# Scale block first, the first chunk's key product in token halves, PSUM as one tile of eight banks, and a new order of work, in a fused attention and token-mixer kernel

## The chip, the core and the metric

The kernel runs on one core of one Trainium2 chip. It is one launch that reads all its inputs from HBM and writes the whole output back. The metric is device microseconds of that launch, the median of several runs; lower is better. The engines named below are PE (matrix products; its weight loads have a row of their own, PEld), DVE (vector work), ACT (activations and copies), POOL (GpSimd) and SP (it issues most DMAs). Each engine works through its own queue strictly in the order in which the program was written; an instruction that waits holds up everything behind it on its engine.

## What is computed

A block of 2048 tokens of width 512 (`x`, bf16) passes two branches. Six modulation rows of 512 come from a conditioning vector: shift `sa`, scale `ca` and gate `ga` for the first branch, `sb`, `cb` and `gb` for the second.

```python
mod = (_silu(c) @ w_mod).reshape(1, 6, 1, -1)      # sa, ca, ga, sb, cb, gb
h = _layernorm(x) * (1 + ca) + sa
# 32 heads of 16; each token sees itself and 7 earlier ones, 2 apart
q, k, v = heads(h @ wqkv)
logits = einsum('bhsd,bhswd->bhsw', q, gathered(k)) * 16 ** -0.5
o = einsum('bhsw,bhswd->bhsd', softmax(masked(logits)), gathered(v))
x = x + ga * (o @ wo)
h = _layernorm(_layernorm(x) * (1 + cb) + sb)
u = gelu(einsum('bsd,sf->bdf', h, w1) + b1)        # mixes tokens, 2048 -> 1792
x = x + gb * transpose(einsum('bdf,fs->bds', u, w2) + b2)
```

## The kernel before

The 2048 tokens are worked in four chunks of 512 (`build_chunk`, chunk number first in the names below), each of four tiles of 128 tokens. For a chunk the steps are:

- `ln1s` and `ln1n`: statistics and normalization of a token tile. `rstd` (ACT) and `nb` (DVE or POOL) lie between them.
- `tr`: PE transposes the normalized tiles into PSUM. `hT` copies them out with the scale `1 + ca` (`a1col`) and the shift `sa` (`sacol`) applied, one per 128 features (kt 0 to 3).
- `qkvq`, `qkvk`, `qkvv`: the three products, each of 16 matmuls of 512 columns; `evq`, `evk`, `evv` copy them to SBUF.
- `qk` (DVE, four big products of 4096 elements per partition), `red` (PE sums them), `max`, `sub`, `exp`, `sum`, `rb`, `smul`: the softmax. `a2` and `a2ev` spread the weights.
- `vd`: 16 SBUF-to-SBUF DMAs make shifted copies of v. `pv` (DVE, four more big products), `pvacc` (PE) and `oev` give the attention output.
- `wo` (PE), `x1ev` (ACT or DVE) and `x1sq` (ACT): output product, residual and its statistics. When `x1ev` runs on ACT, PE adds the residual with a fifth matmul against the identity; on DVE the residual is an operand and four matmuls are enough. The gate `ga` is multiplied into `wo` beforehand by four `gmul`.
- `t`, `aff`, `ln3s`, `h3`: the second pair of normalizations.

The token mixer follows. `mlp1_0` multiplies `w1` with the first two chunks (8 token tiles), `park0` stores the half sums, `mlp1_1` does the last two chunks: its parts ending in `_0` need chunk 2's `h3`, those ending in `_4` chunk 3's. Then come `gadd`, `gelu`, `gbm`, the product `mlp2` with `w2`, `xb` (residual and bias, one per token tile), `fin` and the stores. `modcols` is the product that gives `sa` and `ca` as columns, `modrows` gives the other four rows, `bc` spreads each over the partitions by a DMA, and `biascols` transposes the biases. `warm` are matmuls whose result nobody reads.

The order of all this is written out: `ORDER` (line 27) is one list of names, and the program records each step in that order, so it sets the order in every engine's queue and in SP's. A letter behind a name picks the engine (v is DVE, a is ACT, g is POOL), a digit the PSUM buffer. PSUM is four tiles of two banks (lines 272 to 277). All instructions are recorded through one helper, so the profile's line is L184 for all of them; the tile names tell them apart. `_Graph` (line 98) checks that the order respects the data.

Of the kernel before, what the change touches and what calls it, by code (L numbers as in the profile page):

```python
# [980 lines left out]
```

## Time and profile before

| quantity | value |
|---|---|
| runs | 198.53, 198.63, 199.68 us; median 198.63 |
| span of the profiled execution, first to last instruction | 197.0 us |
| median run less that span | 1.6 us |
| PE busy | 190.1 us (97%), 1289 matmuls |
| DVE busy | 153.5 us (78%), 198 instructions |
| ACT busy | 123.4 us (63%) |
| POOL busy | 18.0 us (9%) |
| granted TensorE clock | 0.998 of full speed over the span |

The profile was taken of one execution, and its only own time is the span; no time with the launch around it is given for that execution apart. Times in the trace count from the span's start. A row of the timeline gives start, length, engine, operation, written tile, read tiles, shapes and how many instructions were merged; in brackets stands the idle time before it and what ended it. Successive instructions overlap by some hundredths of a microsecond, so work in a full queue is counted from start to start. PE's rows overlap more: a matmul of 512 columns lasts 379 ns, but the next starts after 0.215 us.

### The profile page before, as it was taken

How to read it: one execution, taken by the hardware profiler on the slowest of the kernel's cores; microseconds unless marked ns; L12 is line 12 of the kernel's file. 1: busy time of each engine (PE TensorE's matmuls, PEld its weight loads, DVE VectorE, ACT ScalarE, POOL GpSimd, SP SyncE). 2: the span in 40 equal slices, each digit the busy share in tenths (PEclk: the TensorE clock that was granted, in tenths of full speed). 3: DMA queues.
4: the chain of work that ended last, by engine and by line, in shares of the span. 5: the costliest groups of instructions: out<-in, count | busy, mean ns of one | idle time of the engine just before them, and what ended most of it. 6: DMA issues, size and time to landing. Idle time of an engine off the chain costs nothing.

```text
span 197.0 us, 3408 instructions
## 1 busy us (share of the span) xinstructions
PE 190.1 (97%) x1289; PEld 88.2 (45%) x1289; DVE 153.5 (78%) x198; ACT 123.4 (63%) x242; POOL 18.0 (9%) x46
## 2 busy tenths in 40 slices
PE   7889999999999999999999999999999999999994
PEld 2546545445443435433434444444444444444452
DVE  1699989999999999999999999928776127261463
ACT  5498999999999999993769999917541000000000
POOL 7003040090000004300000011000000000000000
PEclk9999999999999999999999999999999999999999
DMA  6999978507994994693999999990000871720112
GB/s 182 369 312 318 302 195 177 120 14 180 171 196 99 270 201 84 187 289 106 174 206 290 234 295 292 292 273 4 0 0 0 229 200 68 199 81 26 57 53 80
DMA packets 45348, 33.59 MB, mean 171 GB/s; under 512 B 5396, under 2 KB 42772, under 8 KB 45332
## 3 DMA queue, kind: packets, MB, share of 16 engines
q1 hardware_dynamic: 44908, 32.82, 67.2%
q10 hardware_dynamic: 424, 0.56, 1.0%
q8 instruction: 10, 0.16, 0.4%
q14 instruction: 6, 0.05, 0.1%
HBM read 22.03 MB, written 2.10 MB: 122 GB/s over the span
## 4 chain that ended last, share of the span: by engine, by line
PE 64%; DVE 12%; DMA 11%; ACT 5%; SPq 3%; issue 2%; ACTq 0%; DVEq 0%
PE ps L184 64%; DMA vD<-v_c 5%; DMA w_q<-in_A_wqkv_dram 4%; SPq L184 3%; DVE pvb L184 3%; DVE prod L184 3%; DMA vD<-in_w_mod_dram 3%; DVE st L184 2%; ACT n_sb L184 1%; DVE h L184 1%; ACT hTb L184 1%; DVE gT L184 1%; ACT v_c L184 1%; DVE ee L184 1%; DVE nm L184 1%
## 5 line engine op out<-in xcount | busy, mean ns | idle before, releaser
L184 DVE TENSOR_TENSOR pvb<-a2sb,vD 128x4096 bf16<-128x4096 bf16 x16 | 36.0, 2284 | 0.2 <-issue 0.2
L184 PE MATMUL ps<-h,wst 128*128 128x512 bf16 x128 | 29.5, 379 | 0.0
L184 DVE TENSOR_TENSOR prod<-q_sb,k_c 128x4096 bf16<-128x4096 bf16 x9 | 20.4, 2285 | 0.1
L184 PEld LDWEIGHTS <-wst 128*128 128x128 bf16 x128 | 12.1, 98 | 16.0 <-issue 1.7
L184 PE MATMUL ps<-gT,vD 128*128 128x512 bf16 x84 | 19.1, 379 | 0.0
L184 PE MATMUL ps<-hTb,w_q 128*128 128x512 bf16 x64 | 15.1, 381 | 1.0 <-DMA w_q<-in_A_wqkv_dram 0.7
L184 DVE TENSOR_TENSOR q_sb<-ps,q_sb 128x512 bf16<-128x512 f32 x8 | 5.4, 687 | 13.6 <-PE ps L184 13.6
L184 PE MATMUL ps<-woq,o_sb 128*128 128x512 bf16 x64 | 15.8, 379 | 0.0
L184 PEld LDWEIGHTS <-w_q 128*128 128x128 bf16 x96 | 9.9, 109 | 12.6 <-issue 2.5
L184 PE MATMUL ps<-hTb,w_v 128*128 128x512 bf16 x64 | 15.0, 380 | 0.0
L184 PE MATMUL ps<-hTb,w_k 128*128 128x512 bf16 x64 | 15.0, 380 | 0.0
L184 DVE TENSOR_TENSOR k_c<-ps,k_c 128x512 bf16<-128x512 f32 (+2 forms) x9 | 5.6, 629 | 11.7 <-PE ps L184 11.7
L184 PEld LDWEIGHTS <-o_sb 128*128 128x128 bf16 x106 | 9.7, 98 | 10.5 <-issue 0.4
L184 PEld LDWEIGHTS <-vD 128*128 128x128 bf16 x116 | 9.2, 97 | 11.4 <-DMA vD<-in_w_mod_dram 1.5
L184 PE MATMUL ps<-gT,pvb 128*128 128x512 bf16 x56 | 12.9, 379 | 0.0
L184 PEld LDWEIGHTS <-w_k 128*128 128x128 bf16 x80 | 8.7, 111 | 8.9 <-issue 0.8
L184 PE MATMUL ps<-gT,prod 128*128 128x512 bf16 x56 | 12.2, 379 | 0.0
L184 PEld LDWEIGHTS <-w_v 128*128 128x128 bf16 x80 | 8.3, 111 | 8.2 <-issue 1.3
L184 ACT ACTIVATE junk<-xx,su 128x512 bf16<-128x512 bf16 x16 | 11.5, 720 | 0.5 <-DVE xx L184 0.2
L184 DVE BATCH_NORM_STATS2 st<-xx 128x6 f32<-128x512 bf16 x11 | 7.4, 671 | 4.7 <-DMA xx<-in_A_x_dram 4.7
L184 ACT ACTIVATE hTb<-ps,sacol,a1col 128x512 bf16<-128x512 bf16 x13 | 9.6, 782 | 0.5 <-PE ps L184 0.5
L184 DVE TENSOR_TENSOR gT<-q_sb,k_c 128x4096 bf16<-128x4096 bf16 x4 | 9.1, 2284 | 0.0
(113 smaller groups left out, 315.1 us busy)
## 6 DMA issues: line engine op xcount, KB each, us to landing
vD<-v_c SPq DMA_DIRECT2D x64, 131.5 KB, 4.6
wst<-in_B_w_dram SPq DMA_DIRECT2D x8, 512.0 KB, 6.1
vD<-in_B_w_dram SPq DMA_DIRECT2D x3, 896.0 KB, 7.3
wst<-in_w_mod_dram SPq DMA_DIRECT2D x4, 512.0 KB, 9.3
prod<-in_B_w_dram SPq DMA_DIRECT2D x2, 896.0 KB, 11.0
pvb<-in_B_w_dram SPq DMA_DIRECT2D x2, 896.0 KB, 8.1
xx<-in_A_x_dram SPq DMA_DIRECT2D x4, 256.0 KB, 4.7
xx<-in_A_x_dram SPq DMA_DIRECT2D x2, 512.0 KB, 7.7
```

Source lines behind the costliest of these rows:

```text
L184: r = fn(*a, **k)
```

## The change

The new kernel computes the same. Its parts:

1. **Scale block first.** The loads of the scale `ca` come right behind the first x tiles (`ld_ca0`, `ld_ca1`, 256 KB each), then the key weights, and the shift `sa` only then (`ld_sa`, 512 KB). Before, shift and scale came together (`ld_wmodA`, `ld_wmodB`, 512 KB each). `modcols` becomes `colsa` and, later, `colss`.
2. **The first chunk's keys.** `hk` copies the transposed tiles out of PSUM with the scale alone, for 256 tokens at a time. The key product of chunk 0 loops over kt outermost and over the two token halves: 8 groups of 4 matmuls of 256 columns, instead of 16 matmuls of 512.
3. **Shift as bias.** `kbias` multiplies the shift with the key weights (16 one-column matmuls); `evk0` adds it while it copies. For queries and values of chunk 0, `hadd` adds the shift to the scaled tiles.
4. **PSUM** is one tile of eight banks. A step takes one bank or two neighbours; before, each took a pair.
5. **New order** of everything, with other engines for some steps. In the table the steps on POOL go from 17 to 25: 7 `ln1n` instead of 5, all 4 `gmul` instead of 1, 4 `t` instead of 3, 5 `h3` instead of 3. `x1ev` goes to ACT 13 times instead of 9. `xb1`, `xb0` and `xb3` move from the end of the program to between the last chunks' steps on DVE. `warm2`, `warm3` and `warm4` (2, 3 and 3 matmuls) now stand among the chunks' products.

On ACT the start reads as follows before: sums of the scale and shift columns out of PSUM, one `hT`, then the statistics of chunk 1.

```order
L184 ACTIVATE lv_0_130<-mv_0_126,epscol 128x2
L184 ACTIVATE rs_0_136<-lv_0_130 128x2
L184 ACTIVATE sacol<-ps_61 128x4
L184 ACTIVATE a1col<-ps_61 128x4
L184 ACTIVATE hTb<-ps_63,sacol,a1col 128x512
L184 ACTIVATE junk,mv_1_127<-xx 128x512
L184 ACTIVATE junk,mv_1_127<-xx,mv_1_127 128x512
```

The same place on ACT in the new kernel (`gT` holds the scaled tiles, `sabf` and `sacol` the shift, `kbcol` the keys' bias):

```order
L187 ACTIVATE n_sb<-xx,nb_0_141,rs_0_135 128x512
L187 ACTIVATE gT<-ps,a1col 128x256 x2
L187 ACTIVATE sabf<-ps 128x4
L187 ACTIVATE sacol<-ps 128x4
L187 ACTIVATE junk,mv_1_126<-xx 128x512
L187 ACTIVATE junk,mv_1_126<-xx,mv_1_126 128x512
L187 ACTIVATE kbcol<-ps 128x4
L187 ACTIVATE hTb<-gT,sacol 128x512
```

The shift's columns come later than before, and between them and the first finished `hTb` tile stand a statistics step of chunk 1 and the copy of the bias.

POOL's queue behind its constants, before (`h_96` and `h_95` are the two chunks' buffers of the second normalization, `h_66` is `h3`):

```order
L184 TENSOR_SCALAR n_sb<-xx,rs_1_137,nb_1_143 128x512 x2
L184 TENSOR_SCALAR n_sb<-xx,rs_0_136,nb_0_142 128x512 x3
L184 TENSOR_TENSOR woq<-woq,ga_bc 128x512
L184 TENSOR_SCALAR h_96<-xx,rs_1_139,nb_1_145 128x512 x3
L184 TENSOR_SCALAR h_66<-h_95,rs_0_140,nb_0_146 128x512 x2
```

And in the new kernel (`h_93`, `h_92` and `h_63` are those three):

```order
L187 TENSOR_SCALAR n_sb<-xx,rs_1_136,nb_1_142 128x512 x3
L187 TENSOR_SCALAR n_sb<-xx,rs_0_135,nb_0_141 128x512 x2
L187 TENSOR_TENSOR woq<-woq,ga_bc 128x512 x4
L187 TENSOR_SCALAR h_93<-xx,rs_1_138,nb_1_144 128x512 x3
L187 TENSOR_SCALAR h_63<-h_92,rs_0_139,nb_0_145 128x512 x2
L187 TENSOR_SCALAR h_92<-xx,rs_0_137,nb_0_143 128x512
```

All four multiplications of `wo` by the gate now stand in POOL's queue, where there was one; three of them left DVE.

On DVE, the stretch around the last `pv` products reads like this before (the products `pvb<-`, three residual sums `xx,su<-`, then the second normalization):

```order
L184 TENSOR_TENSOR ee_83<-ee_83,rb 128x1024
L184 TENSOR_TENSOR pvb<-a2sb_84,vD_92 128x4096
L184 TENSOR_TENSOR pvb<-a2sb_85,vD_90 128x4096 x2
L184 SCALAR_TENSOR_TENSOR xx,su_0_148<-ps_61,xx 128x512
L184 SCALAR_TENSOR_TENSOR xx,su_0_148<-ps_62,xx 128x512
L184 SCALAR_TENSOR_TENSOR xx,su_0_148<-ps_64,xx 128x512
L184 TENSOR_TENSOR pvb<-a2sb_85,vD_91 128x4096
L184 SCALAR_TENSOR_TENSOR nb_0_144<-su_0_148,rs_0_138 128x4
L184 TENSOR_SCALAR h_95<-xx,rs_0_138,nb_0_144 128x512
```

And in the new kernel (`q_sb<-gb_bc` rows are `xb1` and `xb0`, the CAST is `oev2_3`):

```order
L187 TENSOR_TENSOR ee_80<-ee_80,rb 128x1024
L187 SCALAR_TENSOR_TENSOR q_sb_72<-gb_bc,b2col,xx 128x512
L187 CAST o_sb<-ps 128x1024
L187 TENSOR_TENSOR pvb<-a2sb_82,vD_87 128x4096 x2
L187 TENSOR_TENSOR pvb<-a2sb_82,vD_88 128x4096 x2
L187 SCALAR_TENSOR_TENSOR nb_0_143<-su_0_147,rs_0_137 128x4
L187 TENSOR_SCALAR h_92<-xx,rs_0_137,nb_0_143 128x512
L187 SCALAR_TENSOR_TENSOR q_sb_71<-gb_bc,b2col,xx 128x512
```

The three residual sums left DVE there, and two `xb` and one copy out of PSUM joined it.

The diff, cut to its core (of `ORDER` one line on each side):

```diff
-consts ld_x00 consts2 ld_c warm0:0 ld_x02 ld_wmodA act_table ld_wmodB ld_w1a ld_x1a cps:1 warm1:2 ld_w1b silu_exp
+consts ld_c ld_x00 ld_x02 ld_ca0 ld_ca1 act_table ld_wk0 ln1s1:v ld_wk2 consts2 warm0:0 ln1s0:v cps:0 silu_exp warm1:1
...
-    WARM=(4, 4, 4, 5, 4),
+    WARM=(4, 4, 2, 3, 3),
...
-    NPS = 4
-    ps = [psp.tile([P, 2, 512], F32, name=f"ps{i}") for i in range(NPS)]
+    NPS = 8
+    ps = psp.tile([P, NPS, 512], F32, name="ps")
...
+    for kh in range(2):
+        dma(wmodc[1][:, 2 * kh:2 * kh + 2, :], wmod_view[:, 2 * kh:2 * kh + 2, D:2 * D], D * P * 2 * 2, [],
+            vdk[0][2 * kh:2 * kh + 2], f"ld_ca{kh}", "act" if kh == 0 else "sp")
...
+    dma(wmodc[0], wmod_view[:, :, 0:D], KT * D * P * 2, [], vdk[0][4:], "ld_sa")
...
+    mod_cols(1, range(KT), "colsa")
...
+    mod_cols(0, range(KT), "colss")
...
+    def f_kb():
+        for j in range(4):
+            for kt in range(KT):
+                nc.tensor.matmul(bank(sl_kb, 0)[:, j:j + 1], lhsT=_ap(w_p[1][:, kt, j:j + 1], [[4, P]]),
+                                 rhs=sabf[:, kt:kt + 1], start=(kt == 0), stop=(kt == KT - 1), skip_group_check=True)
...
+                if ch == 0:
+                    dst = hraw[:, kt, t0:t1]
+                    alts = [("act", _act(n_, 1), lambda dst=dst, src=src, sc_=sc_: nc.scalar.activation(
+                                dst, src(), ACT.Identity, scale=sc_)),
...
+        if ch == 0:
+            for kt in range(KT):
+                rk_ = [("gT", 2 + kt, g0) for (g0, g1) in parts]
+                G.add_any([("dve", 0.25, lambda kt=kt: nc.vector.tensor_scalar(
+                                hT[:, kt, :], hraw[:, kt, :], sacol[:, kt:kt + 1], None, op0=ALU.add)),
...
+            for (g0, g1) in parts:
+                for kt in range(KT):
+                    def f(kt=kt, g0=g0, g1=g1):
+                        for j in range(4):
+                            nc.tensor.matmul(bank(sk[j], 0)[:, g0 * P:g1 * P], lhsT=_ap(w_p[1][:, kt, j:j + 1], [[4, P]]),
+                                             rhs=hraw[:, kt, g0 * P:g1 * P], start=(kt == 0), stop=(kt == KT - 1))
...
+            for j in range(4):
+                dst = k_c[b][:, j, PAD:PAD + C]
+                G.add_any([("act", _act(C), lambda j=j, dst=dst: nc.scalar.activation(
+                                dst, bank(sk[j], 0), ACT.Identity, bias=kbcol[:, j:j + 1])),
```

299 lines of the change are left out of this document (168 added, 131 removed).

## The prediction, on record before the changed kernel was run

> **What bounds the kernel now.** I read the page first, then the chain of waits, then stretches of time, then the engines' timelines. The page's busy row puts PE at 97%, and DVE's slices are full until the 28th of 40.
>
> ```profile
> PE 190.1 (97%) x1289; PEld 88.2 (45%) x1289; DVE 153.5 (78%) x198; ACT 123.4 (63%) x242; POOL 18.0 (9%) x46
> DVE  1699989999999999999999999928776127261463
> ```
>
> The chain (start, length, what) tells which of the two sets the end: a load until 14.7 us, PE, a mixed middle, and PE again to the end.
>
> ```profile
> 6.71 7.94 DMA w_q<-in_A_wqkv_dram
> ...
> 14.70 19.33 PE ps L184 x145
> ...
> 86.30 106.59 PE ps L184 x585
> ```
>
> The stretches show how full the queues are (length, then PE, PEld, DVE, ACT, POOL busy).
>
> ```profile
> 86.30:128.28 41.98, 41.98 (x284) 17.66 (x284) 40.48 (x58) 34.31 (x68) 1.19 (x3) 1.00 1.02 238
> 128.28:194.09 65.81, 65.81 (x319) 30.51 (x317) 33.79 (x53) 9.91 (x15) 0.00 (x0) 1.00 0.32 89
> 14.70:128.28 113.58, 112.42 (x886) 52.04 (x887) 110.75 (x122) 103.88 (x199) 14.12 (x15) 1.00 0.87 204
> ```
>
> From 14.70 on PE idles only 113.58 - 112.42 = 1.16 us, and after 128.28 not at all. DVE is as full: 110.75 of 113.58. At 128.28 PE starts `mlp1_1`'s parts that need chunk 3's `h3`; DVE has written the last of these 0.56 us earlier:
>
> ```profile
> 126.64 1.08 DVE L184 TENSOR_SCALAR h<-h,mv,rs 128x512 bf16<-128x512 bf16 x3
> 128.28 5.99 PE L184 MATMUL ps<-h,wst 128*128 128x512 bf16 x27
> ```
>
> So 128.28 is a gate with two queues before it, both nearly full. Behind it stand the same 20 groups of `mlp1_1` and the same 16 `mlp2` in both programs, 65.81 us without a gap. The forecast is how far the gate moves: the later of PE's and DVE's arrivals.
>
> **The change, part by part.** The start first.
>
> ```profile
> 5.66 0.69 DVE L184 BATCH_NORM_STATS2 st<-xx 128x6 f32<-128x512 bf16 x1 [1.26 <-DMA xx<-in_A_x_dram]
> 9.81 1.45 DVE L184 TENSOR_SCALAR hTb<-ps,a1col,sacol 128x512 bf16<-128x512 bf16 x3 [1.10 <-PE ps L184]
> 16.67 4.49 DVE L184 TENSOR_TENSOR prod<-q_sb,k_c 128x4096 bf16<-128x4096 bf16 x2
> 6.75 0.55 PE L184 MATMUL ps<-sc,vD 128*128 128x1 bf16 x16 [0.69 <-DMA vD<-in_w_mod_dram]
> 10.40 3.61 PE L184 MATMUL ps<-hTb,w_k 128*128 128x512 bf16 x16
> 14.70 3.65 PE L184 MATMUL ps<-hTb,w_q 128*128 128x512 bf16 x16 [0.69 <-DMA w_q<-in_A_wqkv_dram]
> 10.24 0.62 ACT L184 ACTIVATE junk<-xx 128x512 bf16<-128x512 bf16 x1
> 10.99 0.72 ACT L184 ACTIVATE junk<-xx,mv 128x512 bf16<-128x512 bf16 x1
> 16.44 0.83 ACT L184 ACTIVATE n_sb<-xx,nb,rs 128x512 bf16<-128x512 bf16 x1
> ```
>
> One 512-column matmul costs (3.61 - 0.38) / 15 = 0.215 us, a one-column one 0.025. DVE's new queue has `ln1s3`, whose x landed at 5.66, ahead of the silu product: 5.66 + 0.85 + 0.13 = 6.6. `colsa` (16 x 0.025) and the copy of the scale bring it to 7.3. A 256-column `hk` lies between half of 0.54 and 0.54; I take 0.3, since the width is what is halved. The key product so starts near 7.8, not 10.40. Its 32 half-width matmuls cost the same 3.45, but behind it now stand `colss` and `kbias` (0.4 each), the second half's transposes (0.45) and `biascols` (0.14): PE is free at 12.6. The queries must wait longer, for `hadd`. Tile 2's statistics on ACT take 1.5 from 5.66, then come rstd 0.5 and the norm 0.8: near 8.9, and transposes and `hk` end near 10.2. DVE's queue then has three statistics (2.55) ahead of three `hadd` (0.34 each, as `ln1n` below): 13.8. The query weights have one 512 KB load fewer ahead of them and should be there by 13.1. I put `qkvq0_1` at 13.9 instead of 14.70, a gain of 0.8; its bounds are 12.6 and 15.0. On DVE `evk0_0`, `biascols_cp` and four statistics follow before the first `qk`: 18.0 instead of 16.67, a loss of 1.3.
>
> PE behind 14.70: four more residual matmuls, since `x1ev` goes to ACT 13 times instead of 9: 4 x 0.215 = 0.86. `warm3` and `warm4` add 6 x 0.215 = 1.3; `biascols` left, -0.14. With -0.8 for the start PE arrives at the gate at +1.2, if its 1.16 us of idle stay.
>
> DVE's queue from the first `qk` to the last `h3` is counted by these groups (count, busy, mean ns); start to start is 0.08 less.
>
> ```profile
> L184 DVE BATCH_NORM_STATS2 st<-xx 128x6 f32<-128x512 bf16 x11 | 7.4, 671 | 4.7 <-DMA xx<-in_A_x_dram 4.7
> L184 DVE BATCH_NORM_AGGREGATE mv<-st 128x2 f32<-128x6 f32 x21 | 3.8, 182 | 0.8
> L184 DVE TENSOR_SCALAR n_sb<-xx,mv,rs 128x512 bf16<-128x512 bf16 x5 | 1.9, 418 | 0.0
> L184 DVE SCALAR_TENSOR_TENSOR xx<-ps,xx 128x512 bf16<-128x512 f32 x7 | 4.6, 684 | 0.2
> L184 DVE SCALAR_TENSOR_TENSOR q_sb<-gb_bc,b2col,xx 128x512 f32<-128x512 bf16 x8 | 5.9, 744 | 0.0
> L184 DVE TENSOR_TENSOR h<-ps,gT 128x1024 f32<-128x1024 f32 x3 | 3.7, 1222 | 3.9 <-PE ps L184 3.6 <-ACT gT L184 0.3
> ```
>
> Gone: four `x1ev` 2.4, three `gmul` 1.0, one `ln1s` 0.9, `biascols_cp` 0.2, one `h3` 0.3. Added: three `xb` 2.0, `oev2_3` 1.1 (a copy of 1024 out of PSUM, as the last row), one `ln3s` 0.9, one `ln1n` 0.3, one `t` 0.3. Sum -0.2. What left for ACT is hidden there: ACT is busy 34.31 of 41.98 before the gate.
>
> POOL's new load is the uncertain part. These rows are DVE and POOL around `gmul3`, then around `h3_8`.
>
> ```profile
> 38.97 5.25 POOL L184 TENSOR_TENSOR woq<-woq,ga_bc 128x512 bf16<-128x512 bf16 x1 [10.80 <-DMA ga_bc<-mrow]
> ...
> 117.95 0.77 POOL L184 TENSOR_SCALAR h<-h,rs,nb 128x512 bf16<-128x512 bf16 x1
> 38.72 4.49 DVE L184 TENSOR_TENSOR pvb<-a2sb,vD 128x4096 bf16<-128x4096 bf16 x2
> 43.13 1.22 DVE L184 TENSOR_REDUCE nm<-ps 128x128 bf16<-128x1024 f32 x1
> ...
> 118.19 0.99 DVE L184 TENSOR_SCALAR h<-h,mv,rs 128x512 bf16<-128x512 bf16 x2
> ...
> 120.11 0.73 DVE L184 TENSOR_SCALAR h<-xx,rs,nb 128x512 bf16<-128x512 bf16 x2
> ```
>
> `gmul3` ended at 44.22, 1.0 us after DVE's two `pv` ended at 43.21: it seems to have stood still under them and to have run under `max`, which reads PSUM. The other way round, DVE's pair of `h3` beside POOL's `h3_8` took 0.26 more than the pair at 120.11. So each of the two engines can block the other. The Trainium skill ("SBUF — State Buffer", section "Who interferes with whom") says that the two share a pair of ports, which whoever starts first holds for the whole instruction; both rows agree. It speaks against this change: by it, four `gmul` each stop DVE or are stopped by it.
>
> All four can start once `bc0` has landed, near 31.5 (in the old order at 38.97, and `modrows` now stands 7 us earlier). The product `wo0`, which needs all four, comes up on PE near 53.6: 51.69 below, plus 1.7 and 0.4 for `qkvk2_2` and `a2_1`, which now stand before it, plus 0.65 for `warm3`, minus 0.8.
>
> ```profile
> 51.69 1.03 PE L184 MATMUL ps<-woq,o_sb 128*128 128x512 bf16 x4
> ```
>
> In these 22 us DVE has nine big products, one `max` and some waits for `smul`. Each `gmul` that gets in costs DVE between 0 and 1.0 us, so together 0 to 4.1. `h3_8`'s loss is a third of its length; I take a third here too, 1.4. `t8` went from ACT to POOL, right ahead of `aff2_0`: +0.4 (0 to 0.8).
>
> SP's queue is moved past as well. `bc0` and `bc2` now stand in the middle of the 16 `vd0` transfers and wait for `mrow_ev`, with half of those transfers and two `w1` loads behind them.
>
> ```profile
> vD<-v_c SPq DMA_DIRECT2D x64, 131.5 KB, 4.6
> wst<-in_B_w_dram SPq DMA_DIRECT2D x8, 512.0 KB, 6.1
> ...
> 23.97 7.56 SPq L184 DMA_DIRECT2D vD<-v_c  x12
> ```
>
> Twelve issues take 7.56 us, 0.63 each, and a copy lands 4.6 us later. `vd0_031`, which `pv0_1` needs, is the 18th behind `khalo1`: from 23.4 it is issued by 34.7 and lands by 39.3, and `pv0_1` comes near 41. `vd0_100`, six places on, lands by 43.2, `pv0_2` comes near 44.7. I cost this at nothing; the cover is 1.5 us, and if it is gone `pv0_2` waits, and DVE with it. `ld_w1_1_2` now waits for `mlp1_0_20_4`, eight groups (6.9 us) before the gate, and is needed seven groups (6.0 us) behind it: 12.9 us for a load of 6.1.
>
> Sum for DVE: 1.3 - 0.2 + 1.4 + 0.4 - 0.56 of slack = +2.3; for PE +1.2. The gate moves by 2.3 to 2.4: a span of 199.4 instead of 197.0, and with the 1.6 us between span and median run, 201.0. PSUM in banks, the half-width matmuls and the store order I cost at nothing: PE waited for no free bank behind 14.70 (1.16 us of idle in all).
>
> **Rivals.**
>
> *The four `gmul` hide (not slower).* They fall into DVE's `max` and into waits that DVE has anyway. Then DVE arrives at +0.9 and PE sets the gate at +1.2, or at +0 if `warm3` and `warm4` only fill its idle 1.16: 198.6 to 199.8. It decides if DVE's last `h3` is done before 129. For it: POOL has 22 us for about 4 us of work. Against: DVE is busy 110.75 of 113.58.
>
> *PE stands at `wo0`.* If DVE's back-to-back products leave POOL no entry, one to three `gmul` are open at 53.6. DVE then goes on to `pv1_1`, near 58.5, and stops, because `pvacc1_0`, which frees the next buffer, is behind `wo3` on PE. PE waits until 59.5 to 61.6 and DVE as long again: 6 to 8 us, 205 to 207. For it: `gmul3`'s 4.2 us of standstill. Against: DVE's waits for `smul0` and `smul1` are entries.
>
> *A slow start.* PE idles more between 5 and 9 us than before. If it falls back to the speed of its first matmuls, the key product takes 3.45 us more, and the gate moves by some 3.5: 202 to 203.
>
> ```profile
> 1.41 1.89 PE L184 MATMUL ps<-ident 128*128 128x512 bf16 x4 [1.41 <-POOL onecol L184]
> ```
>
> These took over 0.4 each, later ones 0.215. The Trainium skill ("TensorE: Matmul & The Clock Gate", Part 1) wants an idle window of about 3.4 us for that, and I count no idle stretch beyond 1.7.
>
> *Faster by over 1%.* PE has 112.4 + 2.0 us to do before the gate. With no idle left, `qkvq0_1` would have to start by 11.9, earlier than its bound of 12.6. I see no way but an error in these counts.
>
> "Little work left on GpSimd" is not what the built order shows: POOL's steps rise from 17 to 25.
>
> **How the numbers follow.** About 1%, 2.0 us, is what a measurement of this kernel can tell from no change. The forecast, DVE late at the gate (200.0 to 202.5), gets 0.40; hidden `gmul` 0.30; the stand at `wo0` 0.14; the slow start 0.10; faster 0.06. Within 1% lies the second and a fifth of the first: 0.38. Slower 0.56, faster 0.06. The range 198.2 to 204.0 leaves out the stand and the faster case, 0.20.
>
> **What would show it.** Right: `hTb`'s first query matmul near 13.9, DVE's first `prod` near 18, `woq` rows on POOL longer than 1 us or DVE products with gaps beside them, and PE idle just before `mlp1_1`'s second parts, which begin near 130.6. Wrong: DVE's last `h3` at 128 or earlier, or PE idle at the first `woq` matmul.

## The result, and the profile after

The new kernel takes 205.61 us (median of 4 runs, 205.00 to 205.73) against 198.58 us before (4 runs, 197.97 to 199.68): a ratio of 1.035, with a 95% interval of 1.031 to 1.039. It is slower by 7.0 us; the forecast was 201.0, with a range up to 204.0. The profiled execution of the new kernel is its fastest run, 205.0, with a span of 203.3 against 197.0.

The same stretches of time as before, read in the new kernel (length, then PE, PEld, DVE, ACT, POOL busy, clock, DMA share, GB/s):

```profile
15.02:134.66 119.64, 114.63 (x894) 53.87 (x893) 116.32 (x121) 104.12 (x206) 24.17 (x20) 1.00 0.87 212
134.66:200.47 65.81, 65.81 (x319) 30.50 (x317) 33.30 (x50) 10.70 (x16) 0.00 (x0) 1.00 0.20 57
```

Behind the gate PE has the same 319 matmuls in the same 65.81 us. So the whole loss lies ahead of it: the gate moved from 128.28 to 134.66, by 6.38 us. On PE this splits into 0.32 for the later first query matmul (15.02 instead of 14.70), 2.21 of added work (114.63 instead of 112.42) and 3.85 of added idle time (5.01 instead of 1.16). PE waits now, and mostly for DVE:

```profile
PE ps L187 <- DVE ee L187: 1.2, 1, 1.2
PE ps L187 <- DVE h L187: 1.1, 1, 1.1
PE ps L187 <- DVE nm L187: 0.5, 1, 0.5
```

These are PE's waits between 14 and 60 us, from the list of waits: for `smul0` (`ee`), for `qk1_3` (`h`) and for `max1` (`nm`). Together they are 2.9 of the 5.01 us. Behind them PE waits in three places for ACT, 1.7 us in all; the last of these waits ends at 91.58, where `mlp1_0_60_0` starts. From there to the gate PE waits only once, 0.23 us for ACT at 129.26:

```profile
91.58:134.66 43.08, 42.79 (x287) 18.10 (x287) 40.87 (x54) 31.87 (x68) 3.75 (x6) 1.00 1.01 250
```

So DVE holds PE up between 39 and 49 us, and behind 91.58 PE's queue is full up to the gate. What DVE was doing at the first place stands in the timelines of POOL and DVE:

```profile
32.91 10.59 POOL L187 TENSOR_TENSOR woq<-woq,ga_bc 128x512 bf16<-128x512 bf16 x4 [1.22 <-DMA ga_bc<-mrow]
...
32.34 2.26 DVE L187 TENSOR_TENSOR prod<-q_sb,k_c 128x4096 bf16<-128x4096 bf16 x1
34.52 3.25 DVE L187 TENSOR_TENSOR gT<-q_sb,k_c 128x4096 bf16<-128x4096 bf16 x1
37.68 1.64 DVE L187 TENSOR_TENSOR ee<-ee,rb 128x1024 bf16<-128x1024 bf16 x1
39.24 3.24 DVE L187 TENSOR_TENSOR h<-q_sb,k_c 128x4096 bf16<-128x4096 bf16 x1
42.41 1.11 DVE L187 SCALAR_TENSOR_TENSOR nb<-mv,rs 128x4 f32<-128x4 f32 x1
43.44 4.48 DVE L187 TENSOR_TENSOR pvb<-a2sb,vD 128x4096 bf16<-128x4096 bf16 x2
```

A `qk` takes 2.28 us, `smul` 0.68, `nb` 0.16. Beside the four `gmul` four DVE instructions in a row are longer: 3.25, 1.64, 3.24 and 1.11, that is by 0.97, 0.96, 0.96 and 0.95. As soon as the last `gmul` is done, at 43.50, DVE is at its normal pace again. A DVE instruction whose bar is too long for its form, beside an instruction of POOL, is a wait that no list of waits shows.

The start, on PE (transposes, the first half of the key product, the first query matmuls):

```profile
7.25 1.25 PE L187 MATMUL ps<-ident,n_sb 128*128 128x128 bf16 x8
8.52 1.86 PE L187 MATMUL ps<-gT,w_k 128*128 128x256 bf16 x8
...
15.02 1.24 PE L187 MATMUL ps<-hTb,w_q 128*128 128x512 bf16 x5
```

The next row of PE starts at 10.18, so the eight half-width matmuls take 1.66, or 0.21 each, as much as a full-width one does later. DVE's first `qk` comes at 18.89 instead of 16.67, and its last `h3` ends at 134.53:

```profile
18.89 2.27 DVE L187 TENSOR_TENSOR prod<-q_sb,k_c 128x4096 bf16<-128x4096 bf16 x1
...
133.80 0.73 DVE L187 TENSOR_SCALAR h<-h,mv,rs 128x512 bf16<-128x512 bf16 x2
```

### The profile page after: what moved, and what is told of

Read it like the earlier page. It is cut to its first block, busy times and chain, and to the rows that moved or that the text cites. A ratio compares the mean times of both kernels' runs of the same rounds, so it can differ in the third digit from the quotient of the medians.

```text
span 203.3 us, 3483 instructions
## 1 busy us (share of the span) xinstructions
PE 192.5 (95%) x1320; PEld 92.5 (45%) x1320; DVE 158.3 (78%) x198; ACT 123.9 (61%) x248; POOL 29.7 (15%) x54
## 4 chain that ended last, share of the span: by engine, by line
PE 66%; ACT 15%; DVE 7%; DMA 5%; issue 4%; POOL 1%; SPq 0%; DVEq 0%; ACTq 0%; POOLq 0%
PE ps L187 66%; ACT junk L187 6%; DMA wst<-in_B_w_dram 4%; DVE h L187 2%; ACT lv L187 2%; DVE st L187 2%; ACT v_c L187 1%; DMA xx<-in_A_x_dram 1%; ACT rs L187 1%; ACT xx L187 1%; ACT gT L187 1%; DVE pvb L187 1%; ACT h L187 1%; DVE nb L187 1%; DVE nm L187 1%
## 5 line engine op out<-in xcount | busy, mean ns | idle before, releaser
L187 PEld LDWEIGHTS <-w_k 128*128 128x128 bf16 x112 | 10.8, 114 | 7.6 <-issue 1.5
L187 PE MATMUL ps<-gT,prod 128*128 128x512 bf16 x56 | 12.9, 379 | 0.0
L187 POOL TENSOR_SCALAR h<-xx,rs,nb 128x512 bf16<-128x512 bf16 x4 | 3.2, 800 | 65.0 <-DVE nb L187 65.0
L187 PE MATMUL ps<-hTb,w_k 128*128 128x512 bf16 x48 | 11.4, 380 | 0.0
L187 POOL TENSOR_TENSOR woq<-woq,ga_bc 128x512 bf16<-128x512 bf16 x4 | 10.6, 2676 | 1.2 <-DMA ga_bc<-mrow 1.2
L187 ACT ACTIVATE gT<-ps 128x1024 bf16<-128x1024 f32 x7 | 7.1, 1019 | 5.2 <-PE ps L187 5.2
```

The costliest lines, as they stand in the source:

```text
L187: r = fn(*a, **k)
```

## The experiments

All of them keep the 65.81 us behind the gate, so the gate of a run is its span less 68.6. Ratios are to the kernel before, measured anew with each group of runs (medians 198.27 to 198.58), with 95% intervals; "new" is the new kernel, 205.61. The gate is that of the one profiled execution, the median that of all. The forecasts name the runs by these numbers (e2 is the second).

| run | based on | median us | ratio | gate |
|---|---|---|---|---|
| e1, three `gmul` on DVE | new | 203.98 | 1.027 (1.022 to 1.031) | 133.40 |
| e4, four `gmul` on POOL | before | 199.93 | 1.008 (1.006 to 1.010) | 129.53 |
| e8, `gmul` in halves | new | 204.56 | 1.031 (1.027 to 1.035) | 134.36 |
| e2, longer `warm1` | new | 206.06 | 1.040 (1.036 to 1.044) | 135.25 |
| e6, e2 and `modrows` later | new | 205.69 | 1.037 (1.035 to 1.040) | 135.78 |
| e3, no inner warm matmuls | new | 206.70 | 1.042 (1.038 to 1.046) | 135.56 |
| e5, three `xb` behind the gate | new | 205.66 | 1.037 (1.034 to 1.041) | 135.88 |
| e7, e1 + e5 + e6 | new | 202.11 | 1.023 (1.018 to 1.027) | 131.60 |
| e14, e7 and `khalo1` first | new | 202.72 | 1.020 (1.017 to 1.022) | 132.43 |
| e9, e7, `khalo1` first, `modrows` far behind | new | 205.08 | 1.035 (1.032 to 1.038) | 134.54 |
| e12, e9, fourth `gmul` on DVE, no inner warm | new | 205.65 | 1.035 (1.032 to 1.038) | 134.07 |
| e10, `modrows` early | before | 203.50 | 1.027 (1.024 to 1.031) | 132.54 |
| e11, three `x1ev` on ACT | before | 199.80 | 1.008 (1.006 to 1.011) | 129.20 |
| e17, e7, chunk 3's softmax earlier | new | 203.03 | 1.022 (1.020 to 1.025) | 132.62 |
| e18, e17, fourth `gmul` on DVE, no inner warm | new | 203.52 | 1.026 (1.022 to 1.030) | 132.53 |
| e13, the stretch behind the last `pv` rebuilt | new | 212.30 | 1.070 (1.067 to 1.074) | 143.50 |
| e15, all repairs with e13's | new | 209.33 | 1.057 (1.053 to 1.061) | 141.06 |
| e16, e15 without inner warm | new | 209.34 | 1.054 (1.052 to 1.056) | 138.70 |

The start of one and the same code differs by some tenths to a microsecond from execution to execution (the first query matmul at 14.9 to 15.9 in those runs that leave the new start alone), so one part is best read from DVE's first `qk` on.

### The stops that POOL causes

**e1** puts three of the four `gmul` where the kernel before has them.

```diff
-pv0_3 smul1 khalo2
+pv0_3 gmul0:v gmul2:v gmul1:v smul1 khalo2
...
-gmul2:g gmul1:g vhalo2 pvacc0_3 vd1_031 gmul3:g
+vhalo2 pvacc0_3 vd1_031 gmul3:g
...
-oev0_3:a gmul0:g vd1_111
+oev0_3:a vd1_111
```

> The new kernel with three gmul back on DVE, behind pv0_3 as in the kernel before; gmul3 stays on POOL. Theory A (the four gmul on POOL stop DVE, which lost 0.97, 0.96, 0.96 and 0.95 us on four instructions between 34.5 and 43.5): DVE gets 2.9 us back and pays 3 x 0.34 = 1.0, so the gate moves from 134.66 to about 132.8, and the time from 205.6 to about 203.7; no DVE instruction beside gmul is longer than normal, unless gmul3 alone still stops one (0.96). Theory B (PE's own extra work, 2.2 us, and the start carry the loss; the stops on DVE fall into slack): the time stays within 0.5 of 205.6. Theory C (the order behind the first chunk is at fault): also unchanged, or it moves and is lost again before the gate.

It took 203.98, 1.6 us less, near what Theory A had. POOL's one `gmul` and DVE beside it, then the three on DVE:

```profile
34.38 2.27 POOL L187 TENSOR_TENSOR woq<-woq,ga_bc 128x512 bf16<-128x512 bf16 x1 [2.23 <-DMA ga_bc<-mrow]
35.55 3.24 DVE L187 TENSOR_TENSOR gT<-q_sb,k_c 128x4096 bf16<-128x4096 bf16 x1
...
51.53 1.09 DVE L187 TENSOR_TENSOR woq<-woq,ga_bc 128x512 bf16<-128x512 bf16 x3
```

One stop is left, of 0.96; the others are gone. From DVE's first `qk` to the gate it is 113.96 us instead of 115.77: 1.81 less, where the stops that left, less three `gmul`, are 3.84 - 0.96 - 1.00 = 1.88. So what is won on DVE there, ahead of 91 us, reaches the gate.

**e4** is the other way round: the kernel before with that part alone.

```diff
-gmul3:g gmul0:v gmul2:v gmul1:v qk2_1
+gmul3:g gmul0:g gmul2:g gmul1:g qk2_1
```

> The kernel before with all four gmul on POOL and nothing else changed. Theory A (each gmul on POOL stops DVE for its whole 0.96 us): DVE loses up to 4 x 0.96 = 3.8 and saves 3 x 0.34 = 1.0; with 0.56 us of slack the time goes from 198.6 to 200 to 201.4. Theory B (they hide under DVE's instructions that read PSUM, as gmul3 did here, and under its waits): 197.6 to 198.6. Rival: DVE's products leave POOL no entry, PE stands at the first wo, and the time goes above 203.

```profile
40.56 10.51 POOL L184 TENSOR_TENSOR woq<-woq,ga_bc 128x512 bf16<-128x512 bf16 x4 [12.89 <-DMA ga_bc<-mrow]
...
42.52 1.22 DVE L184 TENSOR_REDUCE nm<-ps 128x128 bf16<-128x1024 f32 x1
43.66 6.39 DVE L184 TENSOR_TENSOR pvb<-a2sb,vD 128x4096 bf16<-128x4096 bf16 x2
49.98 3.24 DVE L184 TENSOR_TENSOR prod<-q_sb,k_c 128x4096 bf16<-128x4096 bf16 x1
```

The first `gmul` ran under `max1`, which keeps its 1.22. The other three stopped `pv0_3`, `pv0_2` (6.39 for the pair, which took 4.48 before) and `qk2_1`: 1.91 + 0.96 = 2.87 in all. From `max0` to the gate it is 102.03 us instead of 100.18: +1.85, which is 2.87 less the 1.01 that the three `gmul` took on DVE. The time rose by 1.6 us. Theory A holds (the time is just below its 200), and the price of one stop is known from both sides.

The Trainium skill ("SBUF — State Buffer", section "Who interferes with whom") says that a reduction on DVE never contends with GpSimd, and that an instruction with two inputs in SBUF does. The trace agrees on both: 1.22 for `max1` beside a `gmul`, and 0.95 to 0.97 more for each instruction that was stopped.

**e8** splits each `gmul` into two instructions of 256 columns.

```diff
-nc.gpsimd.tensor_tensor(woq[:, q_, :], woq[:, q_, :], ga_bc[:], op=ALU.mult)
+[nc.gpsimd.tensor_tensor(
+    woq[:, q_, c:c + D // 2], woq[:, q_, c:c + D // 2], ga_bc[:, c:c + D // 2], op=ALU.mult)
+ for c in (0, D // 2)]
```

> The new kernel with each gmul on POOL split into two instructions of 256 columns. Theory A (POOL waits for one DVE instruction and then runs its own to the end, while DVE waits): eight shorter stops of about 0.5 us on as many DVE instructions, 3.8 to 4 us in all, spread over twice as many instructions, and the same time as before the split, 205.6. Theory B (a stop has a fixed cost per POOL instruction): eight stops of nearly 1 us, about 209. Theory C (short instructions slip in between, so the stops become smaller together): 203 to 204.5.

```profile
34.96 16.49 POOL L187 TENSOR_TENSOR woq<-woq,ga_bc 128x256 bf16<-128x256 bf16 x8 [2.72 <-DMA ga_bc<-mrow]
...
35.65 2.76 DVE L187 TENSOR_TENSOR gT<-q_sb,k_c 128x4096 bf16<-128x4096 bf16 x1
38.33 1.15 DVE L187 TENSOR_TENSOR ee<-ee,rb 128x1024 bf16<-128x1024 bf16 x1
39.41 2.76 DVE L187 TENSOR_TENSOR h<-q_sb,k_c 128x4096 bf16<-128x4096 bf16 x1
42.09 0.62 DVE L187 SCALAR_TENSOR_TENSOR nb<-mv,rs 128x4 f32<-128x4 f32 x1
42.63 4.96 DVE L187 TENSOR_TENSOR pvb<-a2sb,vD 128x4096 bf16<-128x4096 bf16 x2
...
48.65 4.95 DVE L187 TENSOR_TENSOR pvb<-a2sb,vD 128x4096 bf16<-128x4096 bf16 x2
```

A stop of a half costs 0.46 to 0.48, so its price goes by POOL's time, not by the instruction (B falls). Six of the eight stopped DVE (the fifth and the last each within a `pv` pair, 4.96 and 4.95 instead of 4.48), 2.84 us in all instead of 3.84; the other two fell beside `max1`. From DVE's first `qk` to the gate it is 114.81 us instead of 115.77, 0.96 less. The time, 204.56, is at the edge of C's range, but its interval overlaps the new kernel's, so the saving is read from the trace.

### The start

**e2** has eight instead of four matmuls in `warm1`.

```diff
-    WARM=(4, 4, 2, 3, 3),
+    WARM=(4, 8, 2, 3, 3),
```

> The new kernel with eight instead of four matmuls in warm1, as in the kernel before. Theory A (PE's clock was never raised before the key product, since the warm matmuls stopped at 5.2 us): matmuls of 512 columns go from 0.43 to 0.215 us near 5.0, the eight transposes and the first eight half-width key matmuls take half, and the first query matmul comes at about 14.0 instead of 15.02; the gate follows by 0.8 to 1.2, time about 204.6. Theory B (the late query matmul comes from DVE's queue ahead of hadd, whatever PE's speed): qkvq0_1 stays within 0.3 of 15.0 and the time at 205.6. Theory C: the idle of 1.1 us behind the warm matmuls lowers the clock again, and nothing changes although eight were run.

```profile
8.29 0.93 PE L187 MATMUL ps<-gT,w_k 128*128 128x256 bf16 x7 [0.22 <-DVE gT L187]
...
13.97 3.62 PE L187 MATMUL ps<-hTb,w_q 128*128 128x512 bf16 x15
...
27.09 1.04 PE L187 MATMUL ps<-wst,gT 128*32 128x512 bf16 x15 [1.35 <-DMA wst<-in_w_mod_dram]
...
28.67 2.34 DVE L187 TENSOR_TENSOR prod<-q_sb,k_c 128x4096 bf16<-128x4096 bf16 x1 [1.19 <-PE ps L187]
```

The half-width matmuls take 0.11 instead of 0.21, and the first query matmul comes at 13.97. So the slow PE was real, as Theory A had it. And yet the time is 206.06. What was won at 14 is lost at 27: PE stands 1.35 us at `modrows`, whose weights (`wst`) have not landed, the logit sums stand behind it, and DVE's `qk1_0` waits 1.19 for them.

**e6** therefore moves `modrows` behind those sums.

```diff
-evq1_0:a modrows:4 rstd1_2_0
+evq1_0:a rstd1_2_0
...
-red0_0:0 red0_1 mrow_ev vd0_030
+red0_0:0 red0_1 vd0_030
...
-red0_2 red0_3 ln1n11:v
+red0_2 red0_3 modrows:4 mrow_ev ln1n11:v
```

> The second experiment (eight matmuls in warm1) with modrows moved behind red0_3 on PE, so that chunk 0's logit sums do not queue behind a product that waits for its load. Theory A (the microsecond won at the start was lost because modrows stood on PE until its last load landed near 27, and qk1_0 waited for red0): qk1_0 follows qk0_2 without a wait, near 27.5, and the time is about 204.5. Theory B (the start is not what counts; DVE's later work catches up with it anyway): qk1_0 comes earlier, and the time stays within 0.4 of 205.6.

```profile
29.30 2.29 DVE L187 TENSOR_TENSOR prod<-q_sb,k_c 128x4096 bf16<-128x4096 bf16 x1 [2.16 <-DMA k_c<-k_c]
```

`qk1_0` now waits 2.16 us for `khalo1` (`k_c<-k_c`, 16 KB), which was issued at 21.2, behind the last big loads, and had not landed. The time is 205.69: neither A's 204.5 nor B's reason.

**e14** is e7 (below) with `khalo1` issued first.

```diff
-ld_wmod3 ld_wo0 ld_wo1 khalo1
+khalo1 ld_wmod3 ld_wo0 ld_wo1
```

> The seventh experiment with khalo1 issued ahead of ld_wmod3, ld_wo0 and ld_wo1, and nothing else moved on SP or PE. Theory A (qk1_0 waited 1.16 us only because khalo1 stood behind these loads): it starts by 27.4, max0 near 29.6 instead of 30.6, and the time falls by about 1.0, to 201.1. Theory B (the vd copies and modrows, which come when they came, hold the next steps): qk1_0 earlier, pv0_1 or smul0 waits instead, time 202.1 within 0.4.

ACT and DVE behind it:

```profile
29.59 0.69 ACT L187 ACTIVATE mrow<-ps,onecol 128x512 bf16<-128x512 f32 x1 [2.79 <-PE ps L187]
...
35.90 2.29 DVE L187 TENSOR_TENSOR gT<-q_sb,k_c 128x4096 bf16<-128x4096 bf16 x1 [2.52 <-ACT q_sb L187]
```

`qk1_0` comes at 26.97 without a wait. Then ACT stands 2.79 us at `mrow_ev`, behind `modrows` and its load, with chunk 1's `evk1_2` and `evq1_2` in its queue, and `qk1_2` waits 2.52 for these: 202.72 against e7's 202.11, which their scatter does not tell apart. It is B in kind: another wait takes the place of the one removed. **e9** put `modrows` and the `bc` transfers still further behind:

```diff
-ld_wmod3 ld_wo0 ld_wo1 khalo1 vd0_101
+khalo1 ld_wmod3 ld_wo0 ld_wo1 vd0_101
...
-red0_3 modrows:4 mrow_ev ln1n11:v
+red0_3 ln1n11:v
...
-evq1_2:a exp0 ln1n9:g vd0_110
+evq1_2:a modrows:4 exp0 mrow_ev ln1n9:g bc0 vd0_110
```

(`bc2` moved likewise, next to `bc1`.)

> The seventh experiment (three gmul on DVE, the three xb behind the gate, eight matmuls in warm1) with khalo1 issued ahead of the last three loads (ld_wmod3, ld_wo0, ld_wo1) and modrows, with its bc transfers, moved further behind. Theory A (what was won at the start is lost at 27 to 30 us, where chunk 1's first qk and modrows wait for transfers that stand behind the big loads): qk1_0 starts without a wait at about 27.2 instead of 28.30, PE does not wait at modrows, and the gate comes 1.2 to 1.6 earlier than in the seventh, near 130.2; time 200.6 to 201. Theory B (later waits, on ACT's chain, take it back): the time stays within 0.4 of 202.1.

Its waits from 20 to 60 us:

```profile
DVE pvb L187 <- DMA vD<-v_c: 2.4, 2, 2.2
PE ps L187 <- ACT ee L187: 1.9, 1, 1.9
ACT mrow L187 <- PE ps L187: 1.2, 1, 1.2
DVE ee L187 <- ACT rb L187: 1.1, 1, 1.1
```

`qk1_0` at 27.19, as A said, and then more is lost than won: `exp0` and with it `rb` and `smul0` come 1.1 late, and the shifted copies of v, behind `bc0` in SP's queue, 2.4: 205.08. **e12** (e9 with the fourth `gmul` on DVE and `WARM=(4, 8, 0, 0, 0)`) shares these waits (2.6 and 1.1), so its 205.65 says nothing of its own part.

> The ninth experiment with the fourth gmul on DVE too and without the matmuls of warm2, warm3 and warm4. Theory A (no stop by POOL is left, saving 0.96 and costing 0.34; the inner warm matmuls only filled PE's idle time): about 0.6 less than the ninth, near 200. Theory B (PE's work is by now as late as DVE's, so the 1.7 us of warm matmuls count too): 198.5 to 199.3. If the rest of the new order is no better than the old, it stays above 198.6 in both cases.

**e10** puts `modrows` alone into the kernel before, ahead of the sums.

```diff
-qkvq1_0:2 red0_0:1
+qkvq1_0:2 modrows:3 red0_0:1
...
-red0_1 red0_2 red0_3 ln1s13:v
+red0_1 mrow_ev red0_2 red0_3 ln1s13:v
...
-qkvk1_2:0 modrows:2 tr2_10:3 sum0 evk1_2:a mrow_ev rb0
+qkvk1_2:0 tr2_10:3 sum0 evk1_2:a rb0
```

> The kernel before with modrows ahead of red0, where the new kernel has it, and nothing else changed. Theory A (modrows there waits for the last of the first loads, and the logit sums behind it make DVE wait): PE stands 0.5 to 2 us at modrows, max0 comes as much later, and the time rises by 0.5 to 2.0, to 199 to 200.3. Theory B (the loads have landed by then, and the move is free): 198.3 within 0.3.

```profile
ACT mrow L184 <- PE ps L184: 3.6, 1, 3.6
DVE nm L184 <- PE ps L184: 1.8, 1, 1.8
DVE prod L184 <- ACT q_sb L184: 1.7, 1, 1.7
```

```profile
42.05 5.45 DVE L184 TENSOR_TENSOR pvb<-a2sb,vD 128x4096 bf16<-128x4096 bf16 x2
```

`max0` waits 1.8 instead of 0.8 and comes 1.0 later, within the forecast. But ACT also stands 3.6 us at `mrow_ev`, and the copies of q and k behind it make two more `qk` wait, 1.7 and 0.4. And `gmul3`, which ran beside `max1` in the kernel before, now meets other instructions of DVE and stops the first `pv` product (5.45 for the pair instead of 4.49). These make 4.1 of the 4.3 us by which the gate moved. The time rose by 5.2 instead of 0.5 to 2.0: the place of `modrows` decides through ACT's queue and through what POOL meets as well, which I had not counted.

What holds these back is the burst of loads. DMA share and GB/s in the new kernel:

```profile
8.52:15.02 6.50, 6.50 (x76) 5.70 (x76) 5.09 (x17) 4.60 (x16) 0.77 (x1) 1.00 1.10 356
15.02:28.00 12.98, 12.98 (x97) 7.75 (x99) 12.77 (x18) 12.70 (x23) 2.27 (x3) 1.00 1.06 267
28.00:46.00 18.00, 15.66 (x162) 8.21 (x154) 17.95 (x12) 15.52 (x28) 14.28 (x6) 1.00 0.85 211
```

The DMA engines are full up to 28 us. Whatever starts chunk 1's sums needs transfers that land at the end of this burst; in e2, e6 and e7 the microsecond won ahead of it was waited away there (`qk1_0` at 28.67, 29.30 and 28.30, against 28.18 in the new kernel). How late they land differs between executions: in e18, whose `khalo1` stands where e7's does, `qk1_0` came at 27.16 without a wait.

### PE's added work

**e3** takes the eight matmuls of `warm2` to `warm4` out.

```diff
-    WARM=(4, 4, 2, 3, 3),
+    WARM=(4, 4, 0, 0, 0),
```

> The new kernel without the matmuls of warm2, warm3 and warm4 (8 in all, 1.73 us of PE work whose result nobody reads). Theory A (DVE arrives last at the gate, PE has idle time that they only fill): PE idles 1.3 to 1.7 more before the gate and the time moves by less than 0.5. Theory B (PE's own work sets the gate): 1.7 us less, about 203.9.

```profile
14.88:135.56 120.68, 112.64 (x875) 52.51 (x889) 116.59 (x122) 104.50 (x207) 24.78 (x20) 1.00 0.87 209
```

PE's busy time is 2.0 us less, and it idles 8.04 us instead of 5.01 (19 matmuls fewer are recorded, though 8 left, so part of this is missing records). The time, 206.70, is not lower. That is Theory A for these matmuls: the new kernel has them at 14.6, 43.1 and 83.0, and behind the last two PE waits anyway (0.52 at 49.11, 0.83 at 84.64). It says nothing of PE's four added residual matmuls, which stand between 108 and 122, where PE has no wait to fill.

### The stretch behind chunk 2's last products

**e5** moves `xb0`, `xb1` and `xb3` behind the gate.

```diff
-mlp1_0_11_0 xb1 mlp1_0_50_0:0
+mlp1_0_11_0 mlp1_0_50_0:0
...
-t11:v t8:g xb0 oev3_3:a
+t11:v t8:g oev3_3:a
...
-ld_w2_3 xb3 x1sq12
+ld_w2_3 x1sq12
...
-mlp1_1_11_4 gadd1
+mlp1_1_11_4 xb0 gadd1
...
-gbm13
+gbm13 xb1 xb3
```

> The new kernel with xb0, xb1 and xb3 moved behind the gate, near where the kernel before has them. Theory A (DVE arrives last at the gate, so each piece of work that is put ahead of the gate on DVE counts): xb1 0.66 (part of it beside a wait for a2ev3), xb0 1.02 (0.85 where t8 then sets aff2_0), xb3 0.67: the gate comes 1.5 to 2.3 earlier, at 132.4 to 133.2, time about 203.7. Theory B (PE's work or ACT's chain of rstd and x1sq sets the gate): within 0.5 of 205.6.

It did not get faster: 205.66. In the profiled run `modrows` waited 1.55 us for its load, as in e2, and DVE's `qk1_0` 1.75. Of the 2.4 us taken from DVE only 0.7 shows: from the start of `pv2_3` to `aff2_0` it is 15.84 us instead of 16.57. Where `xb1` was, DVE waits 0.75 for PE, and where `xb3` was, 0.42 for ACT. So A falls here: this work lay in waits.

PE's row tells why little could come of it. From `mlp1_0_60_0` on, at 91.58 in the new kernel and 93.34 in e5, PE's steps start at the same distances, within 0.02 us, for 37 us, with and without the three `xb`. To the gate it is 43.08 us there (above) and 42.54 here:

```profile
93.34:135.88 42.54, 42.12 (x282) 18.12 (x288) 39.30 (x52) 31.92 (x68) 3.75 (x6) 1.00 0.99 250
```

PE had no wait for DVE in this stretch that a faster DVE could have taken away; 0.54 is what the three `xb` were worth, and 0.23 of it is the wait for ACT at 129.26. That is Theory B's case, PE's queue being the full one; no run takes work off PE there.

Before, that stretch took 14.34 us. **e11** asks what of it is due to the residual sums, in the kernel before.

```diff
-x1ev10:v
+x1ev10:a
...
-x1ev11:v x1ev9:v
+x1ev11:a x1ev9:a
```

> The kernel before with x1ev9, x1ev10 and x1ev11 on ACT, as in the new kernel, in their old places (PE adds one matmul for each, 0.65 in all; DVE loses 3 x 0.62 of work). Theory A (DVE's sum of work decides, ACT has room): the gate stays or comes up to 0.5 earlier; 198.0 to 198.6. Theory B (behind the last pv the chain wo, x1ev, x1sq, rstd2, t sets when aff2_0 can start, and ACT is in it): aff2_0 comes 0.5 to 1.5 later than 111.44 and the time rises as much.

```profile
106.23 2.29 DVE L184 TENSOR_TENSOR pvb<-a2sb,vD 128x4096 bf16<-128x4096 bf16 x1 [2.67 <-PE ps L184]
110.20 0.16 DVE L184 SCALAR_TENSOR_TENSOR nb<-su,rs 128x4 f32<-128x4 f32 x1 [1.68 <-ACT rs L184]
...
112.94 1.22 DVE L184 TENSOR_TENSOR h<-h,ab_bc 128x2048 bf16<-128x2048 bf16 x1
```

It is 16.40 us now from `pv2_3` (96.54) to `aff2_0`, 2.06 more, and the time rose by 1.5. DVE has 2 us less to do and waits 4 us more: `pv3_2` for PE, `nb2_2_0` for ACT's `rstd2`. Theory B: ACT has room on the average, and none in this chain. The gate feels only part of the 2.06. PE's last wait ahead of this stretch ends at 86.30 in the kernel before and at 85.74 here, and from there to the gate it is 41.98 us and 43.46: 0.65 for the three matmuls that PE adds, 0.62 for one wait for `pv3_3` at 113.07, and 0.2 in small gaps. So PE's added matmuls count here, as much as the chain does.

**e17** is e7 with chunk 3's softmax one product earlier, and `oev2_3` on ACT.

```diff
-mlp1_0_01_4 pv2_1 vd3_000 max3
+mlp1_0_01_4 max3 pv2_1 vd3_000
...
-pvacc2_0:6 pvacc2_1 vd3_110 ld_w1_0_5 vd3_100 sub3
+pvacc2_0:6 sub3 pvacc2_1 vd3_110 ld_w1_0_5 vd3_100 exp3
...
-park0_3:a pv2_3 sum3 rb3 smul3 mlp1_0_11_0
+park0_3:a smul3 pv2_3 a2_3:6 mlp1_0_11_0 a2ev3:a
...
-oev2_3:v
+oev2_3:a
```

> The seventh experiment with chunk 3's softmax one product earlier, as in the kernel before: max3 ahead of pv2_1, sub3 and exp3 ahead of their neighbours, smul3 between pv2_2 and pv2_3, and oev2_3 on ACT. Theory A (behind pv2_3 DVE stands 1.0 us and copies 1.2 us only because a2_3 comes late in the new order): pv3_0 follows pv2_3 within 0.3 us, DVE gets 1.5 to 2.1 us back, and the time falls from 202.1 to 200.0 to 200.6. Theory B (behind it the chain wo, x1ev on ACT, x1sq, rstd2, t sets aff2_0, whatever DVE has done): DVE waits at nb2_2_0 instead, and the time falls by less than 0.6.

```profile
109.79 4.49 DVE L187 TENSOR_TENSOR pvb<-a2sb,vD 128x4096 bf16<-128x4096 bf16 x2 [1.50 <-PE ps L187]
114.59 0.16 DVE L187 SCALAR_TENSOR_TENSOR nb<-su,rs 128x4 f32<-128x4 f32 x1 [0.31 <-ACT rs L187]
```

203.03 against 202.11, and the same ratio to the kernel before (1.022 and 1.023): no gain. `pv3_2` now waits 1.50 for PE, and `nb2_2_0` comes straight behind ACT's `rstd2` as in e7 (0.31 and 0.32). In size that is Theory B. PE again says why: in e7 it runs from `mlp1_0_60_0`, at 89.06, to the gate in 42.54 us, without a wait for DVE; here it stands 0.57 us at `a2_3`, for `smul3`, and takes 43.49. **e18** (fourth `gmul` on DVE, no inner warm matmuls) changed nothing on top of it: 203.52, with a new wait of 1.06 at `qk1_2`.

> The seventeenth with the fourth gmul on DVE and without the matmuls of warm2, warm3 and warm4. Theory A (DVE sets the gate until it meets PE's sum): 0.6 less for gmul3, 199.4 to 200.0, PE's idle time up by the 1.7 us of warm matmuls taken out. Theory B (PE has become the later one): 198.3 to 199.3.

Three runs went wrong in another way. **e13** (on the new kernel, with e5's moves), **e15** and **e16** (on e14, with all four `gmul` on DVE) rebuilt this stretch by hand; in doing so I put `oev3_1` behind the three `t`.

```diff
-wo10:5 park0_1:a x1ev11:a wo9:4 pvacc3_0:2 wo8:6
+wo10:5 park0_1:a x1ev11:v wo9:7 wo8:6 x1ev10:v x1ev9:v pvacc3_0:2
...
-nb2_2_0:v ld_w2_2 t10:a mlp1_0_40_0:2
+nb2_2_0:v t10:a t8:a t9:a oev3_1:a t11:v pv3_3 ld_w2_1 ld_w2_2 mlp1_0_40_0:2
```

> The new kernel with the three xb behind the gate and the stretch around chunk 2's last pv as before: x1ev9 to x1ev11 and t9 on DVE or ACT as in the kernel before, oev2_3 and t8 on ACT. Theory A (behind pv2_3 the chain oev, wo, x1ev, x1sq, rstd2, t sets the time, and the new order lengthened it: aff2_0 starts 14.3 us behind the end of pv2_3's stretch instead of 12.1): aff2_0 comes 1.5 to 2.2 earlier relative to pv2_3 and the gate with it; time 203.4 to 204.2. Theory B (only DVE's sum of work counts there): three residual sums go back to DVE (+1.9), xb and oev2_3 leave (-3.2), so 1.3 earlier at most, and 205.2 or more if the xb alone brought 0.5. Theory C: PE's part sums behind it set the gate, no change.

> All repairs together: all four gmul on DVE, three xb behind the gate, eight matmuls in warm1, modrows behind red0_3, khalo1 ahead of the last loads, and the tail of the thirteenth. Theory A (the losses are these, each on DVE's way to the gate): from the seventh's 202.1, 0.6 for the fourth gmul, 1.0 for khalo1 and 1.0 to 1.5 for the tail: 199.0 to 199.5, within 1% of the kernel before. Theory B (other parts of the new order cost as well): 200.5 or more.

> The fifteenth without the matmuls of warm2, warm3 and warm4. Theory A (DVE still arrives last): within 0.4 of the fifteenth. Theory B (with DVE repaired, PE's 2.2 us of added work set the gate): 0.8 to 1.7 less, at or below the kernel before.

PE in e16, from its timeline and by stretches:

```profile
118.58 1.86 PE L187 MATMUL ps<-h,w_q 128*128 128x512 bf16 x4 [5.29 <-ACT o_sb L187]
```

```profile
118.58:121.89 3.31, 3.31 (x8) 0.99 (x8) 3.21 (x5) 0.00 (x0) 0.00 (x0) 0.54 1.15 289
121.89:125.00 3.11, 3.11 (x27) 1.33 (x27) 0.99 (x4) 2.97 (x5) 0.00 (x0) 1.00 1.19 292
```

The product `mlp1_0_40_0` waits 5.29 us for the banks that `oev3_1` frees, and its eight matmuls then run at half speed. These three say nothing of the tail, and less still of what the repairs add up to.

### Together

**e7** joins e1, e5 and e6.

> The new kernel with three gmul on DVE, the three xb behind the gate, eight matmuls in warm1 and modrows behind red0_3. Theory A (these are separate losses on one queue, DVE's): they add up to 1.9 + 1.9 + 1.0 = 4.8 at most, the gate comes near 130, and PE, with 2.2 us more work than before, becomes as late as DVE: 200.8 to 201.5. Theory B (the order behind the first chunk loses it in other places again): 203 or more.

202.11, 3.5 us less than the new kernel: neither A's 201 nor B's 203. Its gate is 3.3 later than before. In its trace stand, as DVE's own losses against the kernel before: 1.19 for the later first `qk` (17.86), 1.16 and 0.31 for the waits at `qk1_0` and `qk1_2`, 0.56 for the last stop, 1.5 for the stretch to `aff2_0` (15.85 instead of 14.34). That makes 4.7; less work and shorter waits elsewhere give 1.4 of it back. The 1.5 can also be counted on PE, which has no wait for DVE in that stretch and 0.86 us of added residual matmuls in it; no run separates the two. Each of the runs that took one of these away (e14, e17, e18) met another wait close behind it. No version tried beats the kernel before.

## Why the prediction was wrong

- **The gate** was the right frame: 65.81 us behind it in both kernels. The direction was right. How DVE's lateness reaches the gate was not: DVE's last `h3` ends 0.13 us before it instead of 0.56, but PE is not idle there, as the prediction's sign had it. DVE held PE up at 39 to 49 us (2.9 us of waits), and from 91.58 on PE's queue was full.
- **The four `gmul`**: this step failed most. "`h3_8`'s loss is a third of its length; I take a third here too, 1.4." They cost 3.84 (0.95 to 0.97 each), four whole instructions. The row of `h3_8` was the wrong neighbour: there POOL's instruction had begun 0.24 us ahead of DVE's pair (117.95 and 118.19), and only the rest of its 0.77 us could stand in the way; a `gmul` that waits beside DVE and gets in when DVE's instruction ends costs its whole length. The bound from above, 4.1, was right, and by itself would have put the sum at 203.7. e1 and e4 show the price on both kernels.
- **DVE's start**: +1.3 was forecast, +2.2 came (18.89). The rival of the slow start had the right cause: PE ran at half speed (0.21 for a half-width matmul) until about 10.5. But its price, 3.5 at the gate, was wrong: e2 takes the slowness away, brings the first `qk` 0.7 earlier and gains nothing, since `qk1_0` then waits for what the loads hold back. What the whole 2.2 is worth at the gate no run shows.
- **PE's added work**, 0.86 + 1.3 - 0.14 = 2.0, was right in size (2.2 measured). That it does not count holds for the inner warm matmuls (e3). The four residual matmuls, 0.86 of it, stand behind 91.58, where PE has no wait that they could fill; e11 shows three such matmuls counting in the kernel before.
- **DVE's moved work**, -0.2: DVE's way from the first `qk` to the last `h3` grew from 111.05 to 115.64, by 4.59. 3.84 is stops and 0.36 `t8` on POOL beside `xb0` (1.10 instead of 0.74; +0.4 forecast). That leaves 0.4 for the moved work and waits. With 2.2 at the start and 0.4 of slack used up, the sum is 2.2 + 4.6 - 0.4 = 6.4, the gate's shift.
- **"What left for ACT is hidden there"** failed as a reason. e11 shows that three `x1ev` on ACT lengthen the chain behind the last `pv` by 2.06 us. In the new kernel this hardly showed as idle time: `xb0`, `xb1` and `oev2_3` stood there, and where `xb1` left, a wait of 0.75 came (e5). So DVE's sum came out nearly right partly by work that lay in waits, which is luck. That taking DVE work away there (e5, e17) brings little has a second reason: PE's queue is full.
- **PE standing at `wo0`** gave the right time, 205 to 207, for a wrong reason: the `gmul` were done at 43.50, and `wo0` at 57.62 waited for nothing.
- **SP's queue at nothing** was right for the new kernel: DVE waited for no `vD`. The cover is thin: e9, with `bc0` in front of more copies, made DVE wait 2.4 us.
- The range ended at 204.0, since it left out the stand at `wo0`, and no case in it combined the upper bound of the stops with a late start. Those two together, at the measured 3.84 and +2.2, make 204.4; 0.6 for the moved work leads to the 205.0 of the profiled run.

What stays open: why `gmul3` of the kernel before stood through a boundary between two DVE products (41.0) and entered only beside `max1`. In the new kernel a waiting `gmul` got in at the next boundary four times of four, and e4's, e10's and e8's did too. And the 3.3 us that e7's gate is later than the kernel before's are placed in its trace, but no run removed them.

## What to carry to other kernels

Before an elementwise step goes to POOL "because POOL is idle", look at what DVE runs beside it: here nearly every `gmul` that met a DVE instruction with both inputs in SBUF cost DVE its whole POOL time (0.96, against 0.34 had DVE done it itself); beside a reduction out of PSUM it was free. An earlier start was worth nothing here, since the next chunk's first transfers stood at the end of the load burst: look at which row lands last, not at which engine is free. And where two engines are nearly full, find the last wait of one for the other: what is taken off the other behind that point moves the end little. Behind 91.58 PE had no wait for DVE, and 2.4 us taken off DVE there were worth 0.5.
